# Second channel product of six of eight batches by Strassen's block method, with the later part of the kernel's order made anew

## The chip, the cores and the metric

The kernel runs on one core of one Trainium2 chip. The core has a matrix engine (TensorE, PE in the profile; its weight loads are the row PEld), a vector engine (VectorE, DVE), a scalar engine (ScalarE, ACT), a general engine (GpSimd, POOL) and a queue engine that issues transfers (SyncE, SP). They run side by side and wait for one another by semaphores; each works through its own instructions in the order written. Matmuls read SBUF and write PSUM, which has 8 banks of 128 x 512 f32. The metric is the device time of one execution in microseconds; the median of several runs is compared.

## The reference, cut to what matters

```
kv  = einsum('bhsd,bhse->bhde', k, v)       # q, k, v are (8, 8, 576, 64)
out = einsum('bhsd,bhde->bhse', q, kv)
x   = out / sqrt(mean(out*out, -1) + 1e-6) * g_norm     # then heads side by side: (8, 576, 512)

a1  = alpha1 * x + beta1
tok = einsum('ts,bsd->btd', w_tok, a1)      # 576 x 576 over the tokens
u   = x + lam * tok
a2  = alpha2 * u + beta2
ch  = maximum(a2 @ w_ch1, 0) @ w_ch2        # 512 -> 2048 -> 512
out = u + lam * ch                          # f32, (8, 576, 512)
```

The change is in the second factor of `ch`: per batch a product of 576 x 2048 (after the maximum) by 2048 x 512.

## The kernel before, in words

A batch b (0 to 7) has 576 tokens: four full chunks of 128 tokens (c = 0 to 3, the main rows) and 64 left over. The left-over rows of an even batch and of the odd one after it are put together into one chunk of 128 (c = 4, the tail), which is worked with the odd batch.

The stages of a batch, with the lines that the profile names:

- kv (lines 611, 617): per pair of heads, matmuls of k with v in a slow fp32 form; ACT and DVE put the result into `kvc` (628, 630). The q rows are transposed by DVE in `qs` to `qp` (1093) and copied by ACT into `qt` (1096).
- norm (701, five chunks): q times kv, four slow fp32 matmuls each, then ACT squares (669), DVE sums (672), ACT root, DVE reciprocal, and three DVE products of 512 columns (680, 685, 687), the last two into `rm` (bf16, for the token mix) and `xm` (f32, kept).
- tok (784; tail 829): the token mix, five bf16 matmuls of 512 columns per chunk; DVE adds the result to `xm` (794).
- a2: two POOL operations per chunk (874 by alpha2, 881 plus beta2, to bf16 in `a2b`), then a transposing DMA on SP into `a2m` (three buffers).
- ch1 (894): for each of 16 blocks fj of the 2048 features, four matmuls of 512 columns; ACT takes the maximum with 0 into `ht[:, fj, :]` (889). The tail has 64 matmuls of 128 columns (906).
- ch2 (923): for each chunk c, 16 matmuls of 512 columns, with a 128 x 128 block of `ht` as weights and `w2[:, fj, :]` streamed. Then `finish`: DVE multiplies the bank by lam into `tmp` (951), POOL adds it to `xm` (956; on DVE in the last batch), SP stores the rows (960; tail 964). In the last batch, chunk 3 comes last and in three parts of 256, 128 and 128 columns (934), so that little follows the last matmul.

Every operation is made by a call of `P.op`, `P.mm` or `P.dma` and gets a number in the order of the calls. `ORDER` is a written list of these numbers, made by a planner: `replay` puts the operations in this order, and each engine's and each queue's instructions follow it. "722:1" gives the operation's PSUM bank; numbers joined by "+" have their matmuls interleaved one by one (`woven`), which is how the slow fp32 matmuls of attention are set between bf16 ones. `GATES` are extra dependences, mostly for loads. `synchronize` works out the waits. The costs that the planner used are lines of the kernel: VectorE 0.155 us + n/960, ACT 0.175 + n/1200, POOL 0.08 + 2.42 n/1000 for two operands.

POOL also issues the loads of k and v of the next batch (1083, 1087), SP those of q (1075).

Of the kernel before, what the change touches and what calls it, by code (L numbers as in the profile page):

```python
# [6 lines left out]
F32 = mybir.dt.float32  # L7
F32R = mybir.dt.float32r
# [16 lines left out]
13 0 3 6 30 4 31 ~32 14 7 1 32 12 9 28 5 8 208 10 36 11 27 21 37 35 20 34 29 19 49 43:1 48 ~5 18  # L25
26 16 50:2 25 15 17 2 52:4 56:5:6 51 ~3 57 53 44 23 54:3 45:7 58 62 59 22 63 60 64 55 61 65
127:1 46 73:4:5 38 128 66:2:3 74 42 129 80:6 75 67 190 137:1:7 24 189 81 68 76 191 77 138 82 69
192 130 70 78 40 83 39 ~2 71 135:5 79 143 131:4 139 136 144 140 133:2 145 84 141 85 132 87:5 88
~3 146 99:6 86 142 111:3 112 134 33 113 100 101 114 105:7 106 89 207 102 196 93:4 94 116 107 90
# [1175 lines left out]
```

## Time and profile before

| | us |
|---|---|
| runs | 343.48, 345.99, 346.15 |
| median | 345.99 |
| span of the profiled execution, first to last instruction | 341.3 |
| TensorE busy in it | 332.7 |

For the profiled execution the span is what is given; the times of runs hold what lies around the span, too. In the rows of groups, a line reads: line of the kernel, engine, operation, output <- inputs, shapes, count; then busy time in us and the mean ns of one; then the idle time of the engine before them, and what ended it. A mean of matmuls includes the run through the array, which overlaps the next matmul's, so the pitch from start to start is shorter than the mean. In a timeline or a chain, a line begins with its start and its length in us. In a table by stretch, a line reads: stretch, length, busy time (and count) of PE, PEld, DVE, ACT and POOL, the granted clock of TensorE, the DMA share and GB/s.

### The profile page before, as it was taken

The page shows a single profiled execution, that of the slowest core. Times are in us where ns is not written, and L with a number is a line of the kernel's source. Part 1 is how long each engine was busy: PE and PEld are TensorE (multiplying, and loading weights), DVE is VectorE, ACT ScalarE, POOL GpSimd, SP SyncE. Part 2 cuts the span into 40 slices and gives each one's busy share as a digit, 9 for nine tenths or more (in the row PEclk, how much of TensorE's full clock was granted, in tenths as well). Part 3 has the DMA queues.
Part 4 walks back from the last instruction along what each step waited for, and adds up shares of the span by engine and source line. Part 5 has one row for each costly group of instructions (what it writes and reads, how often), then busy time and mean ns, then how long its engine had stood idle before and what let it go on. Part 6 is the DMA issues. An engine that isn't in the chain of part 4 may idle for free.

```text
span 341.3 us, 5403 instructions
## 1 busy us (share of the span) xinstructions
PE 332.7 (97%) x2141; PEld 191.0 (56%) x2177; DVE 185.9 (54%) x346; ACT 148.8 (44%) x302; POOL 162.3 (48%) x154
## 2 busy tenths in 40 slices
PE   7999999999999999999999999999999999999996
PEld 7776653556555544555655555554576444444644
DVE  3694098424985796365744794458624963210044
ACT  5763663148603680336503572336325472026400
POOL 3699057572039608761087706932292607930000
PEclk9999999999999999999999999999999999999999
DMA  7999999999913991379723995399407530330013
GB/s 261 304 271 230 211 197 298 121 139 276 119 35 62 243 215 23 93 168 236 136 33 76 257 197 72 95 138 246 79 0 125 187 105 17 77 129 12 0 63 92
DMA packets 108496, 48.10 MB, mean 141 GB/s; under 512 B 82029, under 2 KB 101557, under 8 KB 108472
## 3 DMA queue, kind: packets, MB, share of 16 engines
q1 hardware_dynamic: 81648, 26.38, 40.6%
q0 software_dynamic: 26800, 21.38, 39.5%
q8 instruction: 17, 0.28, 0.4%
q14 instruction: 7, 0.06, 0.1%
q10 hardware_dynamic: 24, 0.01, 0.0%
HBM read 38.82 MB, written 9.44 MB: 141 GB/s over the span
## 4 chain that ended last, share of the span: by engine, by line
PE 79%; DVE 8%; DMA 4%; ACT 3%; SPq 2%; POOL 2%; issue 1%
PE ps L923 32%; PE ps L894 26%; PE ps L784 8%; PE ps L906 3%; DMA qs<-in_q_dram 3%; PE ps L701 2%; PE ps L611 2%; POOL a2b L881 2%; DMA w<-in_k_dram 1%; DVE ps L680 1%; DVE small L672 1%; PE ps L829 1%; SPq L1075 1%; PE ps L934 1%; PE ps L567 1%
## 5 line engine op out<-in xcount | busy, mean ns | idle before, releaser
L923 PE MATMUL ps<-w,hh 128*128 128x512 bf16 x543 | 134.1, 382 | 0.8 <-issue 0.2
L894 PE MATMUL ps<-a2m,w 128*128 128x512 bf16 x498 | 120.4, 381 | 0.6
L889 ACT ACTIVATE hh<-ps 128x512 bf16<-128x512 f32 x144 | 80.9, 598 | 71.0 <-PE ps L894 58.3
L923 PEld LDWEIGHTS ps<-w,hh 128*128 128x128 bf16 x560 | 48.2, 98 | 50.1 <-issue 0.8
L894 PEld LDWEIGHTS ps<-a2m,w 128*128 128x128 bf16 x512 | 46.5, 98 | 51.3 <-ACT hh L889 1.3
L874 POOL TENSOR_TENSOR a1f<-xm,a_bc 128x512 f32<-128x512 f32 x24 | 30.3, 1270 | 81.4 <-DVE xm L794 81.1
L951 DVE TENSOR_TENSOR tmp<-ps,lam_bc 128x512 f32<-128x512 f32 (+2 forms) x38 | 24.6, 658 | 52.6 <-PE ps L923 46.4
L956 POOL TENSOR_TENSOR xm<-xm,tmp 128x512 f32<-128x512 f32 x28 | 35.3, 1270 | 28.0 <-DVE tmp L951 28.0
L701 PE MATMUL ps<-kvc,qt 128*128 128x128 f32 x140 | 47.7, 406 | 0.7 <-ACT qt L1096 0.7
L881 POOL TENSOR_TENSOR a2b<-a1f,b_bc 128x512 bf16<-128x512 f32 x32 | 40.2, 1270 | 2.7 <-DVE a1f L878 1.8
L611 PE MATMUL ps<-vr,kr 128*128 128x128 f32 x112 | 38.2, 408 | 0.0
L672 DVE TENSOR_REDUCE small<-sq 128x8 f32<-128x512 f32 (+1 forms) x35 | 23.5, 677 | 24.5 <-ACT sq L669 24.0
L701 PEld LDWEIGHTS ps<-kvc,qt 128*128 128x128 f32 x140 | 27.4, 196 | 8.8 <-ACT qt L1096 0.9
L1096 ACT ACTIVATE qt<-qp 128x576 fp32r<-128x576 f32 x24 | 15.9, 679 | 36.9 <-DVE qp L1093 36.9
L669 ACT ACTIVATE sq<-ps 128x512 f32<-128x512 f32 (+1 forms) x35 | 20.5, 594 | 22.7 <-PE ps L701 22.6
L784 PE MATMUL ps<-rm,wt 128*128 128x512 bf16 x109 | 29.3, 381 | 0.9 <-DVE rtl L685 0.7
L794 DVE TENSOR_TENSOR xm<-ps,xm 128x512 f32<-128x512 f32 x24 | 16.3, 688 | 24.4 <-PE ps L784 23.4
L1093 DVE STREAM_TRANSPOSE qp<-qs 128x576 f32<-128x576 f32 x24 | 18.1, 765 | 13.2 <-ACT qt L1096 8.5
L611 PEld LDWEIGHTS ps<-vr,kr 128*128 128x128 f32 x112 | 22.0, 196 | 5.5
L680 DVE TENSOR_TENSOR ps<-ps,small 128x512 f32<-128x512 f32 (+1 forms) x35 | 23.8, 692 | 0.5
L687 DVE TENSOR_TENSOR xm<-ps,g_bc 128x512 f32<-128x512 f32 x28 | 18.6, 677 | 0.2
L906 PEld LDWEIGHTS ps<-a2l,w 128*128 128x128 bf16 x256 | 15.9, 98 | 3.8 <-ACT hh L889 0.2
(125 smaller groups left out, 295.7 us busy)
## 6 DMA issues: line engine op xcount, KB each, us to landing
out_dram<-xm SPq DMA_DIRECT2D x31, 256.0 KB, 2.7
kr<-in_k_dram POOLq DMA_DIRECT2D x7, 1024.0 KB, 8.2
vr<-in_v_dram POOLq DMA_DIRECT2D x7, 1024.0 KB, 10.0
qs<-in_q_dram SPq DMA_DIRECT2D x24, 288.0 KB, 7.2
w<-in_moe_w_ch_dram POOLq DMA_DIRECT2D x8, 512.0 KB, 9.4
xm<-in_q_dram SPq DMA_DIRECT2D x8, 288.0 KB, 5.2
qs<-in_v_dram SPq DMA_DIRECT2D x4, 288.0 KB, 5.5
w<-in_k_dram SPq DMA_DIRECT2D x4, 288.0 KB, 5.6
```

Source lines behind the costliest of these rows:

```text
L611: P.mm("fill", 128, [lambda e, t=t, c=c, h=h, o=128 * (h % 4): e.matmul(t.ap()[:, o:o + 128], kr4[:, h, c:c + 2, :].rearrange("p c d -> p ...
L672: P.op("DVE", dve(n), lambda e: e.tensor_reduce(out=st, in_=sq[rs, s3, 0:nst, :], axis=AX.X, op=ALU.add), r=[("sq", s3)], w=[("sm", s4)])
L680: P.op("DVE", dve(n), lambda e: e.tensor_tensor(out=grp(ps()), in0=grp(ps()), in1=st[..., None].to_broadcast([rs.stop - rs.start, nst, DH] ...
L701: P.mm("fill", 128, [lambda e, p=p: e.matmul(dst(p), qt[:, p, cs], kvc[:, i, p, :], start=(p == 0), stop=(p == 3)) for p in range(4)], r=[ ...
L784: P.mm("fill", 512, [lambda e, sc=sc: e.matmul(t.ap(), wt[:, sc if sc < 4 else tw(b), 128 * c:128 * c + 128], rsrc(b, sc, al), start=(sc = ...
L874: P.op("POOL", pool(512), lambda e: e.tensor_tensor(out=a1f[:, s], in0=x, in1=a2_bc[:], op=ALU.mult), r=ks + ["a2"], w=[("a1f", s)])
L881: P.op("POOL", pool(512), lambda e: e.tensor_tensor(out=a2b[:, c], in0=a1f[:, s], in1=b2_bc[:], op=ALU.add), r=[("a1f", s), "b2"], w=[("a2 ...
L889: P.op("ACT", act(512), lambda e: e.activation(dst, t.ap(), ACT.Relu), r=[t], w=keys, pri=-1000)
L894: P.mm("main", 512, [lambda e, dj=dj: e.matmul(t.ap(), w1[:, dj, 128 * fj:128 * fj + 128], a2m[:, b % 3, dj, :], start=(dj == 0), stop=(dj ...
L906: P.mm("main", 128, [lambda e, dj=dj, fj=fj: e.matmul(t.ap()[:, 128 * fj:128 * fj + 128], w1[:, dj, 128 * (f4 + fj):128 * (f4 + fj) + 128] ...
L923: P.mm("main", 512, [lambda e, fj=fj, t=t, c=c: e.matmul(t.ap(), (ht[:, fj, 128 * c:128 * c + 128] if c < 4 else hl[:, fj, :]), w2[:, fj, ...
L956: lambda e: e.tensor_tensor(out=x, in0=x, in1=tmp[:, s, a:z], op=ALU.add),
```

## The change

For b = 2 to 7 the main rows of `ch2` are made by Strassen's method in the form with seven products. `ht` (features x tokens) is cut into A11, A21, A12, A22: features 0 to 1023 or 1024 to 2047, tokens 0 to 255 or 256 to 511. `w2` is cut into B11, B21, B12, B22: features by output columns 0 to 255 or 256 to 511. Each product is 16 matmuls of 256 columns (two token chunks by eight feature blocks), in two halves g = 0, 1 of eight matmuls. In the texts they are P1 to P7, in the order of the program:

| | weights x streamed | bank | what follows |
|---|---|---|---|
| P1 | A11 x B11 | ta | ACT copies it to `tmp` |
| P2 | A12 x B21 | tb | DVE adds the copy: rows 0 to 255, columns 0 to 255 |
| P3 | hs x ws2 | ta, on top of P1 | ACT copies it |
| P4 | A11' x t1 | tc | ACT copies it |
| P5 | A21' x B12' | ta, on top | DVE adds the copy of P4: rows 256 to 511, columns 256 to 511 |
| P6 | A12' x B22 | tc, on top of P4 | DVE adds the copy of P3: rows 0 to 255, columns 256 to 511 |
| P7 | A22 x ws1 | ta, on top | DVE multiplies by lam: rows 256 to 511, columns 0 to 255 |

The sums are DVE operations, two halves each, in place but for `hs`: A21(g) = A21 - A11, hs(g) = A22 + A21, and after P1 and P2 have read the old values ("late" sums) A11(g) = hs + A11 and A12(g) = A12 - hs. The sums of weights (t1, ws2, ws1, and B12 - B22 in place of B12) are made once, at b = 2 (`weight_sums`, eight operations); the order puts most of them earlier, in the time of batches 0 and 1. Each operand is 128 x 1024 bf16.

POOL does two operations (times lam, plus `xm`) for three of the four blocks and one for the fourth. Since B12 is changed, the tail of b = 3, 5, 7 is made as 16 matmuls by columns 0 to 255 and 16 by the rest, with one DVE sum of the two halves of `hl` between; in b = 7 the tail comes last of all and takes over the split into 256, 128 and 128 columns. For b from 2 on, ch1 runs its blocks in the order 0, 8, 1, 9, ....

To make room, `a2m` has two buffers for three, `a1f` one for two (after the first mixes), `hs` lies over small tables used at the start, `qt` loses 64 columns of zeros, and t1 lies half in `la_bc`, which is free by then.

Operation numbers after, for reading the order: weight sums 642 to 649; ch1 of b = 2 650 to 681, its Strassen part 682 to 721; for b = 3 Strassen 859 to 898 and the tail 899 to 911; for b = 4 ch1 1002 to 1033, Strassen 1034 to 1073; token mix and a2 of batch 5 977 to 1001; b = 5 Strassen 1211 to 1250; b = 6 1378 to 1417; b = 7 1470 to 1509 and the tail 1510 to 1534. Within a Strassen part the numbers run: A21(0), hs(0), A21(1), hs(1), P1 (two), copy, P2 (two), A11(0), A12(0), A11(1), A12(1), add, POOL (two), P3 (two), copy, P4 (two), copy, P5 (two), add, POOL (two), P6 (two), add, POOL (two), stores, P7 (two), product with lam, POOL, stores.

The core of the diff; of the order, the part around batch 4's Strassen products:

```diff
...
+1078+1028:2 1027 967 975 1030:1 1079 1029 976 977:0 1081 1080 1031 1082 1034 982:7 978 987:3 1085
+979 983 1086 992:2 988 980 1089 997:6 993 984 1090 981 1083 1032:5 998 985 1084 1038:1 1035 1033
+1087 989 1039 986 1036 1088 1041:4 1043 990 1040 1037 1042 1044 994 991 1050 1046 1051 1047 995
+1045 1053:0 1052 999 996 1054 1048 1056 1055 1057 1000 1061 1058 1049 1001 1062 1068 1059 1063
+1069 1064 1099:7+1159:3 1070 1091 1107:2+1161:6 1100 1092 1160 1101 1115:5+1163:4 1108 1093 1102
...
+        def both(op, out, in0, in1, r, w):
+            P.op("DVE", dve(in0.shape[1] * in0.shape[2], 2), lambda e: e.tensor_tensor(
+                out=out, in0=in0, in1=in1, op=op), r=r, w=w)
...
+                t1g = ws4[:] if g else la4
+                both(ALU.subtract, t1g, B12[:, j], B11[:, j], [lo4], [("t1", g)])
+                both(ALU.subtract, ws2[:, j], B22[:, j], t1g, [hi4, ("t1", g)], [("t2", g)])
+                both(ALU.subtract, ws1[:, j], B21[:, j], ws2[:, j], [hi4, ("t2", g)], [("t4", g)])
+                both(ALU.subtract, B12[:, j], B12[:, j], B22[:, j], [lo4, hi4], [lo4])
+
+        def sums(g):
+
+            j = slice(4 * g, 4 * g + 4)
+            both(ALU.subtract, A21[:, j], A21[:, j], A11[:, j], four(g, 0, 0), four(g, 0, 1))
+            both(ALU.add, hs[:, j], A22[:, j], A21[:, j], four(g, 1, 1) + four(g, 0, 1),
+                 [("hs", g)])
+
+        def sums_late(g):
+
+            j = slice(4 * g, 4 * g + 4)
+            both(ALU.add, A11[:, j], hs[:, j], A11[:, j], [("hs", g)], four(g, 0, 0))
+            both(ALU.subtract, A12[:, j], A12[:, j], hs[:, j], [("hs", g)], four(g, 1, 0))
+
+        def product(t, first, at, rhs, keys, stop):
+
+            for g in range(2):
+                P.mm("main", 256, [lambda e, c=c, fj=fj: e.matmul(
+                    t.ap()[:, 256 * c:256 * c + 256], at[:, fj, 128 * c:128 * c + 128], rhs(fj),
+                    start=(first and fj == 0 and c == 0), stop=(stop and fj == 7),
+                    skip_group_check=True)
+                    for c in range(2) for fj in range(4 * g, 4 * g + 4)],
+                    r=keys(g), w=[t])
...
+            js = [8 * m + i for i in range(8) for m in range(2)]
+            for fj in range(4, 16) if b == 0 else range(16) if b == 1 else js:
                 ch1(b, fj)
...
+            else:
+                strassen(b)
+                if b % 2:
+                    ch2_tail(b)
```

More of the change, by code (lines that the diff above doesn't have):

```diff
@@ L527, in e1_rows @@
             P.mm("fill", 4 * DH, [lambda e: e.matmul(
-                tg.ap()[:, 0:DH], one[:], row(4, DH), start=True, stop=True)],
+                tg.ap()[:, 0:DH], one[:], grow, start=True, stop=True)],
                 r=["one", ("row", 4)], w=[tg], tile=4)
@@ L915, in ch2 @@
             tiles = {}
-            if b == NB - 1:
-                order, late = order[:-4], order[-1][0]
             for c, n in order:
@@ L926, in ch2 @@
                     for fj in range(4 * n, 4 * n + 4)],
-                    r=[("w2", n)] + [(hk, fj) for fj in range(4 * n, 4 * n + 4)], w=[t])
+                    r=[("w2", n)] + [("h", fj, c // 2) if c < 4 else ("hl", fj)
+                                     for fj in range(4 * n, 4 * n + 4)], w=[t])
                 if n == 3:
                     finish(b, c, t)
-            if b == NB - 1:
-                for a, z in ((0, 256), (256, 384), (384, 512)):
-                    t = P.bank("main")
-                    for n in range(4):
-                        P.mm("main", z - a, [lambda e, fj=fj, t=t, a=a, z=z: e.matmul(
-                            t.ap()[:, 0:z - a], ht[:, fj, 128 * late:128 * late + 128],
-                            w2[:, fj, a:z], start=(fj == 0), stop=(fj == 15))
-                            for fj in range(4 * n, 4 * n + 4)],
-                            r=[("w2", n)] + [("h", fj) for fj in range(4 * n, 4 * n + 4)],
-                            w=[t])
-                    finish(b, late, t, a, z)
+        A11, A21, A12, A22 = ht[:, 0:8, 0:256], ht[:, 0:8, 256:512], ht[:, 8:16, 0:256], ht[:, 8:16, 256:512]
@@ new lines, in ch2_tail @@
+        def ch2_tail(b):
+            hk = [("hl", fj) for fj in range(16)]
+            t = P.bank("main")
+            for n in range(4):
+                P.mm("main", 256, [lambda e, fj=fj, t=t: e.matmul(
+                    t.ap()[:, 0:256], hl[:, fj, :], w2[:, fj, 0:256], start=(fj == 0),
+                    stop=(b == NB - 1 and fj == 15)) for fj in range(4 * n, 4 * n + 4)],
+                    r=[("w2", n)] + hk[4 * n:4 * n + 4], w=[t])
+            both(ALU.add, hl[:, 8:16], hl[:, 8:16], hl[:, 0:8], hk[0:8], hk[8:16])
+            last = b == NB - 1
+            if last:
+                finish(b, 4, t, 0, 256)
+            for a, z in ((256, 384), (384, 512)) if last else ((256, 512),):
+                o = a
+                if last:
+                    t, o = P.bank("main"), 0
+                for n in range(4):
+                    P.mm("main", z - a, [lambda e, fj=fj, t=t, a=a, z=z, o=o: e.matmul(
+                        t.ap()[:, o:o + z - a], hl[:, fj, :],
+                        w2[:, fj, a:z], start=(last and fj == 0),
+                        stop=(fj == 15)) for fj in range(4 * n, 4 * n + 4)],
+                        r=[("w2", n)] + hk[4 * n:4 * n + 4], w=[t])
+                if last:
+                    finish(b, 4, t, a, z)
+            if not last:
+                finish(b, 4, t)
@@ L1052, in bass_transnormer_attn__then__resmlp_affine_kernel @@
         rws = [("row", i) for i in range(6)]
-        alias([("a2m", i, c) for i in (1, 2) for c in range(4)], rws)
+        alias([("a2m", 1, c) for c in range(4)], rws)
         P.readers.setdefault(("a2m", 0, 0), [])
@@ L1161, in bass_transnormer_attn__then__resmlp_affine_kernel @@
                     ch1(b, fj, ts[fj], [3])
-            for fj in range(0 if b else 4, 16):
+            if b == 2:
+                alias([("t1", 0)], ["la"])
+                alias([("hs", i) for i in range(2)],
+                      rws + [("row", 4), ("cst", 0), ("cst", 1), ("a1f", 1)])
+                weight_sums()
+            js = [8 * m + i for i in range(8) for m in range(2)]
+            for fj in range(4, 16) if b == 0 else range(16) if b == 1 else js:
                 ch1(b, fj)
```

153 lines of the change are left out of this document (118 added, 35 removed), and 140 rows, old and new, of tables (GATES, ORDER).

## The prediction

> **What bounds the kernel now.** The page of the profile comes first, for the busy time of each engine and the chain that ended last; then busy time by stretch, each about one batch long.
>
> ```profile
> span 341.3 us, 5403 instructions
> PE 332.7 (97%) x2141; PEld 191.0 (56%) x2177; DVE 185.9 (54%) x346; ACT 148.8 (44%) x302; POOL 162.3 (48%) x154
> PE 79%; DVE 8%; DMA 4%; ACT 3%; SPq 2%; POOL 2%; issue 1%
> ```
> ```profile
> 74.00:112.00 38.00, 37.08 (x246) 22.21 (x249) 24.17 (x44) 18.34 (x38) 17.48 (x16) 1.00 0.99 125
> ...
> 150.00:188.00 38.00, 37.75 (x247) 22.27 (x251) 21.44 (x38) 17.51 (x36) 18.62 (x17) 1.00 0.81 124
> 188.00:226.00 38.00, 37.90 (x209) 20.51 (x212) 23.58 (x41) 17.22 (x34) 21.48 (x19) 1.00 0.93 152
> ```
>
> TensorE is busy 97% of the span and 99% of the middle stretches (37.75 of 38), at full clock (the 1.00). So columns that TensorE need not stream come off the time one for one, as long as it isn't made to wait. In the same stretches VectorE works 21 to 24 us of 38 and GpSimd 18 to 21: they have room on average, and the question is what they do to the order's tight places. The sum starts from this execution; its 341.3 us lie 4.7 below the median of the runs (345.99), and I carry those 4.7 along as what lies around the span.
>
> **TensorE's work.** The pitch of each shape is read in the chain of waits, where nothing but TensorE stands for long pieces.
>
> ```profile
> 303.76 8.63 PE ps L894 x40
> ...
> 317.58 3.57 PE ps L906 x64
> ...
> 334.96 3.55 PE ps L934 x48
> ```
> ```profile
> L934 PEld LDWEIGHTS ps<-w,hh 128*128 128x128 bf16 x48 | 3.4, 98 | 0.4
> ...
> L934 PE MATMUL ps<-w,hh 128*128 128x128 bf16 x32 | 1.9, 219 | 0.0
> L934 PE MATMUL ps<-w,hh 128*128 128x256 bf16 x16 | 1.9, 272 | 0.0
> ```
>
> 512 columns: 8.63/40 = 0.2158 us. 128 columns: 3.57/64 = 0.0558. Line 934 mixes 32 matmuls of 128 columns with 16 of 256: 3.55 - 32 x 0.0558 = 1.765, so 0.1103 each. Two of 256 cost 0.2206 against 0.2158 for one of 512; the 98 ns weight load fits under one of 256, and no row gives a reason for more.
>
> For a batch b = 2 to 7 the main rows take 64 x 0.2158 = 13.81 us now and 7 x 16 x 0.1103 = 12.35 after: 1.46 less, six times 8.76. The tails of b = 3 and 5 become 32 x 0.1103 = 3.53 for 16 x 0.2158 = 3.45: 0.16 back in all. In b = 7 the split last tile moves from rows to the tail: 48 x 0.2158 + 3.45 + 3.55 = 17.36 before, 12.35 + 3.55 = 15.90 after, the same 1.46. Sum: -8.6 us. The fp32 matmuls of attention were woven one to one or one to two with 512-column matmuls; after, always one to one, with the first product or the token mix, never with a block product:
>
> ```profile
> 177.28 0.39 PE L923 MATMUL ps<-w,hh 128*128 128x512 bf16 x1
> ...
> 177.57 0.39 PE L923 MATMUL ps<-w,hh 128*128 128x512 bf16 x1
> ```
>
> One to one, a pair takes 0.29, so the fp32 matmul costs 0.29 - 0.216 = 0.07 and one partner covers it: nothing changes.
>
> **The new sums on VectorE.** Eight more operations per batch (two operands of 128 x 1024 bf16, both in SBUF), three for the odd tails, eight once for the weights.
>
> ```profile
> L956 POOL TENSOR_TENSOR xm<-xm,tmp 128x512 f32<-128x512 f32 x28 | 35.3, 1270 | 28.0 <-DVE tmp L951 28.0
> L951 DVE TENSOR_TENSOR tmp<-ps,lam_bc 128x512 f32<-128x512 f32 x35 | 23.6, 685 | 51.9 <-PE ps L923 46.4 <-remote 2.9 <-POOL xm L956 2.6
> L1093 DVE STREAM_TRANSPOSE qp<-qs 128x576 f32<-128x576 f32 x24 | 18.1, 765 | 13.2 <-ACT qt L1096 8.5 <-DMA qs<-in_q_dram 4.6
> L794 DVE TENSOR_TENSOR xm<-ps,xm 128x512 f32<-128x512 f32 x24 | 16.3, 688 | 24.4 <-PE ps L784 23.4 <-remote 1.0
> ...
> L956 DVE TENSOR_TENSOR xm<-xm,tmp 128x512 f32<-128x512 f32 x3 | 2.1, 692 | 0.1
> ```
> ```profile
> 336.75 0.43 DVE L951 TENSOR_TENSOR tmp<-ps,lam_bc 128x256 f32<-128x256 f32 x1 [0.33 <-PE ps L934]
> ```
>
> No bf16 pair is in the trace. If a 16-bit element costs what a 32-bit one does, 256 to 512 elements adding 0.26 (0.43 to 0.69), 1024 take 0.69 + 0.52 = 1.2 us; if bytes count, they take as long as 512 of f32, 0.69. I take 0.69: the last group above is the only one with both operands in SBUF, and its bytes are the same. The Trainium skill, VectorE: DVE Perf Modes, § The perf-mode tier table, also has 16-bit pairs in SBUF at two elements a cycle; no run here shows it yet. So VectorE gets 8 x 0.69 = 5.5 us more a batch: some 29 of now 36.5.
>
> Does TensorE wait for them? I walked the order by hand through the places where it is tight. Further rows:
>
> ```profile
> 289.85 0.86 PE ps L829 x8
> ```
> ```profile
> 97.08 2.16 PE ps L784 x10
> ```
>
> Batch b = 4, from the start of tok(5, 0): four token tiles of five matmuls at 0.216 (1.08 each) to 4.32; their tail, ten at 0.86/8, to 5.40; the last ch1 group to 6.26; P1 8.02, P2 9.79, P3 11.55, first half of P4 12.43. An operation that reads a bank starts some 0.16 behind the matmuls' slots (272 ns less the 110 of the pitch). VectorE, in the order's sequence: from 1.28 on without a pause the adds of the four token tiles and three transposes (4 x 0.69 + 3 x 0.77) to 6.35, tail add 7.04, hs(0) 7.73, transpose 8.50, A21(1) 9.19, A11(0) 9.88, hs(1) 10.57, A12(0), A12(1) 11.95, the add after P2 12.6, A11(1) 13.3. P3's second half wants hs(1) at 10.67: there. P4's second half wants A11(1) at 12.43: 0.9 late. The same walk gives 0.7 in b = 3 (hs(1)), 0.8 in b = 5 (A11(1)), about nothing in b = 2 (0.1 to spare) and none in 6 and 7, where A11(1) has microseconds in hand. Sum: +2.5 us, with a lower end of nothing, since tenths in my walk decide.
>
> **Other additions.**
>
> ```profile
> L889 ACT ACTIVATE hh<-ps 128x512 bf16<-128x512 f32 x144 | 80.9, 598 | 71.0 <-PE ps L894 58.3 <-PE ps L906 12.2
> ```
> ```profile
> qs<-in_q_dram SPq DMA_DIRECT2D x24, 288.0 KB, 7.2
> ```
>
> Three ACT copies a batch (0.6 each): a product that writes over the copied bank comes one product later, and 1.77 us of matmuls cover the copy; without that cover each would cost some 0.8. GpSimd runs 7 elementwise operations a batch for 4, +3 x 1.27 = 3.8 us, 23 of 36.5. Behind them on GpSimd are the a2 operations of the next mix and the loads of k and v; behind the stores on SP's queue stand the q loads for the next batch, which the order needs some 15 us later and which take 7.2: nothing. Two a2m buffers for three: their former readers, ch1 of two batches before, ended earlier: nothing. Weight sums:
>
> ```profile
> 55.61 0.70 DVE L797 TENSOR_TENSOR ps<-ps,xm 128x512 f32<-128x512 f32 x1 [0.74 <-PE ps L784]
> ...
> 65.64 0.69 DVE L951 TENSOR_TENSOR tmp<-ps,lam_bc 128x512 f32<-128x512 f32 x1 [2.90 <-remote]
> ```
>
> One stands in the hole of 0.74, four (2.8) in the hole of 2.9, the others later: nothing, and up to 1.4 if they hold up GpSimd's chain there.
>
> **The end.**
>
> ```profile
> 337.61 2.08 SPq L960 DMA_DIRECT2D out_dram<-xm  x4
> ...
> 338.86 0.29 DVE L956 TENSOR_TENSOR xm<-xm,tmp 128x128 f32<-128x128 f32 x1
> ```
>
> SP takes 2.08/4 = 0.52 to issue a store. Now one store follows the last add; after, three (both halves of the last slice and one left over): +1.0.
>
> Total: 341.3 - 8.6 + 2.5 + 1.0 = 336.2, and 4.7 around it: **341 us**.
>
> **Rivals.** First, and on the other side: a VectorE operation with both operands in SBUF and a GpSimd operation cannot read SBUF together, and each waits for the other to end. Before, VectorE's operations beside GpSimd have one operand in SBUF:
>
> ```profile
> 214.93 0.65 DVE L794 TENSOR_TENSOR xm<-ps,xm 128x512 f32<-128x512 f32 x1
> ...
> 214.96 1.27 POOL L881 TENSOR_TENSOR a2b<-a1f,b_bc 128x512 bf16<-128x512 f32 x1
> ```
>
> Neither is longer than its group's mean (0.69, 1.27). The only operations with two are line 956's on VectorE, at the end, when GpSimd has no work left: the trace says nothing against this rival. Where the walk above is tight, GpSimd has 10 to 17 operations of 1.27 in a row (a2 of the next mix, then the adds). There a sum would first wait 0.6 on average, and a whole 1.27 when it follows another sum. In b = 4 seven sums stand on the path to A11(1): 3 x 0.6 + 4 x 1.27 = 6.9 more; b = 2 has two and two (3.7), b = 5 three and two (4.3), b = 3 three and one (3.1). That is +18 where GpSimd is always busy, +11 at its mean share of 23/36.5: 352 to 359, I take 355. It decides once a sum waits over 0.5 us on average, for then some 19 waits eat the 8.6. The Trainium skill, SBUF — State Buffer, § Who interferes with whom, speaks for it: a VectorE instruction with two SBUF inputs contends with a GpSimd instruction that reads SBUF, and the second to start blocks until the first ends.
>
> Second: bf16 sums take 1.2 us. 0.51 more on each late sum: 1.9 in b = 2, 2.3 in 3, 3.6 in 4, 2.6 in 5, so 341 + 10.4 = 351. Third: the order hides all of the sums and the end: 341 - 3.5 = 337.5.
>
> **How the numbers follow.** The sum as made, with the small waits: 0.38, 338.5 to 344. All hidden (third rival): 0.12, 337 to 338.5. GpSimd and VectorE in each other's way (first): 0.38, 345 to 361, since the one row with two SBUF operands was taken with GpSimd at rest, which leaves it as open as the sum. Slow bf16 (second): 0.12, 347 to 355, since the nearest row prices by bytes. About 1% (3.5 us: 342.5 and 349.5) is what this measurement can tell from no change. Faster: 0.30 of the sum as made, all 0.12 of the third rival and 0.02 of the first, 0.44; within: 0.08 of the sum, 0.06 of the first and 0.02 of the second, 0.16; slower: 0.30 of the first and 0.10 of the second, 0.40. The signs are nearly even; the sum as made and the third rival, which is its lower end, hold half the chance, so 341 stands, with 337 to 344 as its own range. The range over all cases is 337 to 357: it leaves out the upper part of the first rival, some 0.13, and a few in a hundred below.
>
> **What would show it.** Pitch: 16 matmuls of a block product start 0.110 apart. Sums: a mean near 690 ns, and near 690 too for those beside GpSimd; the first rival shows in sums of 1.3 to 2 us there, with gaps of TensorE of 3 to 7 us in b = 2 to 5 whose releaser is a sum; the second in 1.2 us for all of them, also in b = 7 where GpSimd rests. TensorE's idle time in the middle stretches tells the waits: 0.1 to 0.9 us now. Wrong I am above all if one place of the order, which I walked by means, hangs on another step.

## The result, and the profile after

| | median, us | runs | ratio to before, 95% interval |
|---|---|---|---|
| before, measured beside it | 345.47 | | |
| after | 360.56 | 358.59 to 363.0 (4) | 1.0454, 1.0397 to 1.0512 |

The ratio compares means of runs; two of the ten runs of `one_operand` below, 348.52 and 351.82, are left out of its ratio and its median span as slow ones. The change makes the kernel 4.5% slower. 341 was forecast, with 337 to 357 as the range; the first rival had 352 to 359.

The page of the profile after: the span, busy time by engine, and the chain that ended last.

```profile
span 358.5 us, 6172 instructions
...
PE 330.6 (92%) x2469; PEld 223.4 (62%) x2497; DVE 238.5 (67%) x400; ACT 159.6 (45%) x320; POOL 201.3 (56%) x176
...
PE 38%; DVE 17%; DMA 16%; POOL 15%; SPq 7%; issue 3%; ACT 2%; POOLq 0%; DVEq 0%
```

TensorE had 79% of the chain before and has 38% now; VectorE and GpSimd, which had 10% between them, have 32%. TensorE's idle time is 28 us of the span where it was 9. Busy time by stretch, three of the seven from 74 to 340 us:

```profile
112.00:150.00 38.00, 35.52 (x240) 23.37 (x242) 32.11 (x50) 17.14 (x33) 25.81 (x21) 1.00 0.96 167
150.00:188.00 38.00, 33.85 (x262) 23.87 (x264) 30.36 (x47) 19.84 (x40) 24.46 (x20) 1.00 0.84 136
...
226.00:264.00 38.00, 35.81 (x228) 23.91 (x230) 28.68 (x47) 16.25 (x33) 23.07 (x19) 0.91 0.76 133
```

Two things are new here. TensorE stands idle 2 to 4 us in every stretch from 112 us on, and in the last one shown its granted clock, 1.00 throughout before, has a mean of 0.91. VectorE and GpSimd are busier than the added operations account for: over the span VectorE's busy time grew by 52.6 us for 54 more operations, which at 0.69 are 37, and GpSimd's by 39.0 for 22 more, which at 1.27 are 28. The block sums are all on line 945. Minimum, median and maximum of one in ns, by form, for batches 2 to 7 (the first row has the three sums of the tails too); then how long TensorE's matmuls waited for them, us and times:

```profile
L945 DVE TENSOR_TENSOR hh<-hh x15: 642/692/1665, 128.2 to 352.0; 128x1024 bf16<-128x1024 bf16 x15
L945 DVE TENSOR_TENSOR hs<-hh x12: 682/692/1746, 130.2 to 334.8; 128x1024 bf16<-128x1024 bf16 x12
L945 DVE TENSOR_TENSOR hh<-hs,hh x12: 676/1455/1768, 139.0 to 336.0; 128x1024 bf16<-128x1024 bf16 x12
L945 DVE TENSOR_TENSOR hh<-hh,hs x12: 669/1172/1764, 141.4 to 338.2; 128x1024 bf16<-128x1024 bf16 x12
...
  PE ps L978: 9.5, 4
```

One operation on one shape takes anything from 0.64 to 1.77 us. The timeline of batch 3 shows when it is long:

```profile
181.39 1.72 POOL L890 TENSOR_TENSOR a2b<-a1f,b_bc 128x512 bf16<-128x512 f32 x1
...
181.91 1.75 DVE L945 TENSOR_TENSOR hs<-hh 128x1024 bf16<-128x1024 bf16 x1
...
183.18 1.59 POOL L883 TENSOR_TENSOR a1f<-xm,a_bc 128x512 f32<-128x512 f32 x1
183.69 1.64 DVE L945 TENSOR_TENSOR hh<-hs,hh 128x1024 bf16<-128x1024 bf16 x1
...
183.71 1.05 PE L978 MATMUL ps<-ws,hs 128*128 128x256 bf16 x8 [2.01 <-DVE hs L945]
...
184.74 1.71 POOL L1007 TENSOR_TENSOR xm<-xm,tmp 128x512 f32<-128x512 f32 x1
```

VectorE and GpSimd are both busy without a pause, and their operations end by turns: a GpSimd operation at 183.11, the sum beside it at 183.66, the next GpSimd operation at 184.77, the next sum at 185.33. From one end to the next it is 0.55, 1.11 and 0.56 us, less than the 0.68 and 1.27 that a sum and a GpSimd operation take undisturbed, but counted from their own starts the operations last 1.6 to 1.75. TensorE's third product wants hs(1) at 181.7 and gets it at 183.7. The like happens in batch 2 (a wait of 1.99), batch 4 (2.08, and 1.77 for a copy that was held up) and batch 5 (3.38), and not in 6 and 7. Batch 7 has a wait of another kind: its first matmul of ch1 waits 2.05 at 320 us for the transposing transfer of the mix, four of whose GpSimd operations took 1.60 to 1.68. In `one_operand` below that wait is 0.4.

In batch 4 the clock comes on top (stretch, length, busy time of PE and the others; the third number from the end is the granted clock):

```profile
222.50:225.00 2.50, 0.84 (x8) 0.50 (x6) 2.50 (x4) 1.12 (x2) 2.34 (x3) 1.00 0.25 52
225.00:227.50 2.50, 1.05 (x8) 0.70 (x8) 2.50 (x2) 0.05 (x1) 2.42 (x2) 0.97 0.26 52
227.50:230.00 2.50, 1.77 (x9) 1.28 (x10) 2.50 (x3) 0.00 (x0) 1.72 (x2) 0.50 0.27 56
230.00:232.50 2.50, 2.50 (x13) 1.56 (x12) 1.64 (x3) 0.60 (x1) 1.38 (x1) 0.50 0.00 0
```

Five microseconds with TensorE busy for 1.9, and then it gets half its clock for some 6 to 7: 13 matmuls in 2.5 us where full speed gives 22. That costs about another 3. The clock falls a second time behind the wait of 3.38 in batch 5 (a mean of 0.67 from 270 to 275 us), for about 1.6.

Two smaller differences, the end and the loads of k and v for batch 5:

```profile
353.08 3.68 SPq L1115 DMA_DIRECT2D out_dram<-xt  x6
...
354.28 0.29 DVE L1107 TENSOR_TENSOR xt<-xt,tmp 128x128 f32<-128x128 f32 x1
```
```profile
156.20 0.92 POOL L1234 DMA_DIRECT2D vr<-in_v_dram  x1
...
166.00 0.30 PE L618 MATMUL ps<-vr,kr 128*128 128x128 f32 x1 [2.02 <-ACT small L682]
```

From the last add to the end of the span it is 358.5 - 354.57 = 3.9 us; before, 341.3 - 339.15 = 2.2. And the key and value product of batch 5 waits 2.0. The releaser named, a root on ScalarE, had ended at 165.0; the load of v issued at 156.20 takes 9.7 us to land, which is 165.9, and the product begins at 166.0. Before, the loads of that batch were issued from 152.8 on and their product began at 171.9.

### The profile page after: what moved, and what is told of

Same layout as the page of the kernel before. It is cut to its first block, busy times and chain, and to the rows that moved or that the text cites. A ratio compares the mean times of both kernels' runs of the same rounds, so it can differ in the third digit from the quotient of the medians.

```text
span 358.5 us, 6172 instructions
## 1 busy us (share of the span) xinstructions
PE 330.6 (92%) x2469; PEld 223.4 (62%) x2497; DVE 238.5 (67%) x400; ACT 159.6 (45%) x320; POOL 201.3 (56%) x176
## 4 chain that ended last, share of the span: by engine, by line
PE 38%; DVE 17%; DMA 16%; POOL 15%; SPq 7%; issue 3%; ACT 2%; POOLq 0%; DVEq 0%
PE ps L903 15%; PE ps L978 10%; DMA qs<-in_q_dram 7%; POOL a2b L890 6%; DVE hh L945 4%; POOL a1f L883 4%; DMA vr<-in_v_dram 3%; SPq L1111 3%; SPq L1226 3%; DVE qp L1244 3%; PE ps L792 2%; PE ps L929 2%; DMA w<-in_moe_w_ch_dram 2%; PE ps L915 2%; DMA a2m<-a2b 2%
## 5 line engine op out<-in xcount | busy, mean ns | idle before, releaser
L903 PE MATMUL ps<-a2m,w 128*128 128x512 bf16 x495 | 126.3, 384 | 4.0 <-DMA a2m<-a2b 2.0
L978 PE MATMUL ps<-w,hh 128*128 128x256 bf16 x384 | 46.0, 278 | 0.1
L709 PE MATMUL ps<-kvc,qt 128*128 128x128 f32 (+1 forms) x140 | 42.6, 406 | 0.9 <-ACT qt L1247 0.9
L978 PEld LDWEIGHTS ps<-w,hh 128*128 128x128 bf16 x384 | 38.1, 100 | 7.7 <-issue 0.8
L1004 POOL TENSOR_TENSOR tmp<-tmp,lam_bc 128x512 f32<-128x512 f32 x18 | 24.5, 1361 | 21.8 <-DVE tmp L1016 21.8
L929 PE MATMUL ps<-w,hh 128*128 128x512 bf16 x139 | 34.7, 382 | 0.2
L679 DVE TENSOR_REDUCE small<-sq 128x8 f32<-128x512 f32 (+1 forms) x35 | 23.3, 674 | 13.1 <-ACT sq L676 12.8
L709 PEld LDWEIGHTS ps<-kvc,qt 128*128 128x128 f32 (+1 forms) x140 | 27.2, 195 | 3.0 <-ACT qt L1247 1.1
L1012 ACT ACTIVATE tmp<-ps 128x512 f32<-128x512 f32 x18 | 10.7, 595 | 40.2 <-PE ps L978 40.2
L1016 DVE TENSOR_TENSOR tmp<-ps,tmp 128x512 f32<-128x512 f32 x18 | 12.3, 683 | 24.5 <-PE ps L978 24.5
L978 PE MATMUL ps<-ws,hh 128*128 128x256 bf16 x144 | 19.2, 287 | 5.4 <-DVE hh L945 5.4
```

What stands on the lines that cost most here:

```text
L709: P.mm("fill", 128, [lambda e, p=p: e.matmul(dst(p), qt[:, p, cs], kvc[:, i, p, :], start=(p == 0), stop=(p == 3)) for p in range(4)], r=[ ...
L903: P.mm("main", 512, [lambda e, dj=dj: e.matmul(t.ap(), w1[:, dj, 128 * fj:128 * fj + 128], a2m[:, b % 2, dj, :], start=(dj == 0), stop=(dj ...
L929: P.mm("main", 512, [lambda e, fj=fj, t=t, c=c: e.matmul(t.ap(), (ht[:, fj, 128 * c:128 * c + 128] if c < 4 else hl[:, fj, :]), w2[:, fj, ...
L978: P.mm("main", 256, [lambda e, c=c, fj=fj: e.matmul(t.ap()[:, 256 * c:256 * c + 256], at[:, fj, 128 * c:128 * c + 128], rhs(fj), start=(fi ...
L1004: P.op("POOL", pool(512), lambda e: e.tensor_tensor(out=two(tmp[:, s]), in0=two(tmp[:, s]), in1=lam(f), op=ALU.mult), r=[("tmp", s), "lam" ...
```

## The experiments

The theory after this reading: two-operand sums on VectorE and GpSimd's operations exclude each other, and this is nearly all of the loss. Against it: the sums are late by the order itself; GpSimd's three more operations a batch are what hurts; the clock fell for its own reason.

### Is it an exclusion at all

`lock_alone` computes nothing of the reference: phases of twelve operations on VectorE, on GpSimd, or both at once.

```diff
+phase(lambda e, i: e.tensor_tensor(out=dc[:, i], in0=da[:], in1=db[:], op=TT), None)
+phase(None, lambda e, i: e.tensor_tensor(out=pc[:, i], in0=pa[:], in1=pb[:], op=TT))
+phase(lambda e, i: e.tensor_tensor(out=dc[:, i], in0=da[:], in1=db[:], op=TT),
+      lambda e, i: e.tensor_tensor(out=pc[:, i], in0=pa[:], in1=pb[:], op=TT))
...
```

> A kernel of its own that measures the disputed thing by itself and leaves the computation out: eight stretches of 12 operations on VectorE and 12 on GpSimd, which start together. Theory (two SBUF operands of VectorE and the reads of GpSimd exclude each other): a bf16 sum takes 0.69 us alone and 1.4 to 1.8 beside GpSimd's two-operand operations, which go from 1.27 to about 1.7; the same for an f32 sum of 512; a sum with one operand in PSUM and a reduction stay at 0.69 and 0.67 and leave GpSimd at 1.27; beside a fill on GpSimd, which reads nothing, the sum stays at 0.69; beside a copy of one operand it is stretched. Rival (plain shortage of SBUF bandwidth): every VectorE operation beside GpSimd is stretched by some tenth, whatever its operands. Rival (nothing of its own; the stretching comes from semaphores in the kernel): 0.69 and 1.27 everywhere.

By line: the sum alone, a GpSimd operation alone, both at once (two rows), then the sum with one operand in PSUM beside GpSimd, the sum beside a GpSimd fill, and beside a GpSimd copy.

```profile
L311 DVE TENSOR_TENSOR dc<-da,db x12: 680/681/692, 6.2 to 12.8; 128x1024 bf16<-128x1024 bf16 x12
L312 POOL TENSOR_TENSOR gb<-pa,pb x12: 1259/1260/1262, 13.5 to 26.9; 128x512 f32<-128x512 f32 x12
L313 DVE TENSOR_TENSOR dc<-da,db x12: 692/1743/1750, 28.2 to 45.5; 128x1024 bf16<-128x1024 bf16 x12
L314 POOL TENSOR_TENSOR gb<-pa,pb x12: 1706/1706/1766, 28.3 to 46.7; 128x512 f32<-128x512 f32 x12
L315 DVE TENSOR_TENSOR dc<-ps,fb x12: 677/677/691, 48.4 to 55.0; 128x512 f32<-128x512 f32 x12
...
L319 DVE TENSOR_TENSOR dc<-da,db x12: 681/683/692, 83.4 to 90.0; 128x1024 bf16<-128x1024 bf16 x12
...
L321 DVE TENSOR_TENSOR dc<-da,db x12: 691/1519/1522, 94.2 to 109.2; 128x1024 bf16<-128x1024 bf16 x12
```

Side by side both engines go at about 1.7 us an operation: 12 pairs in 20.2 us, hardly better than one after the other (12 x 1.94 = 23.3). With one operand in PSUM, or beside a GpSimd operation that reads nothing, the sum is as fast as alone; beside a copy, which reads one input, it takes 1.52. So it is two SBUF inputs against GpSimd's reads, and each is held up by the other. That two f32 inputs of 512 columns fare the same (1.744) shows that it is not a matter of bf16.

### How much of the loss it is

`one_operand` puts a reduction of the same length and with one SBUF input in the place of each of the 48 sums. The sums are left out by that, so the products take the blocks as they are. `thin_pool` keeps the sums and has GpSimd's elementwise operations from batch 2 on work on 8 of the 512 columns; `thin_pool_before` does the same to the kernel before.

```diff
-            both(ALU.subtract, A21[:, j], A21[:, j], A11[:, j], four(g, 0, 0), four(g, 0, 1))
+            one_in(hw[:, 0:8, 128:256][:, j], four(g, 0, 0), four(g, 0, 1))
...
+            P.op("DVE", dve(512), lambda e: e.tensor_reduce(
+                out=scr[:, i], in_=src, axis=AX.X, op=ALU.max), r=r, w=w)
```
```diff
+            nn = 512 if b < 2 else 8
...
-                out=a2b[:, c], in0=a1, in1=b2_bc[:], op=ALU.add),
+                out=a2b[:, c, 0:nn], in0=a1[:, 0:nn], in1=b2_bc[:, 0:nn], op=ALU.add),
```

> The changed kernel with each of the 48 sums of ht replaced by a reduction over the same block read as 512 f32 (one operand in SBUF, 0.67 us, the length that the sum has alone); P3 takes A22 for hs. The sums are so left out; waits, order and GpSimd's work are as in the changed kernel. Theory (exclusion of two-operand reads): no operation is stretched, 340 to 345 us, as the forecast's own sum had it. Rival (VectorE is simply too full, and the order's places too tight, whatever an operation reads): 355 to 361, as the changed kernel. In between, 346 to 354, both have a part.

> The changed kernel with GpSimd's elementwise operations from batch 2 on cut from 512 columns to 8 (a2, the product with lam, the adds to xm; the other columns are left out). Theory: with next to nothing to collide with, the sums take 0.69, and the time is 337 to 343. Rival (VectorE too full): 354 to 361, since VectorE has as much to do as before.

> The control: the kernel before with the same cut of GpSimd's operations from batch 2 on. Both theories: 343 to 347, since TensorE is busy 99% there and waits for GpSimd nowhere; if it comes out below 342, GpSimd's operations cost time before as well, and the run of the changed kernel with the same cut has to be read against this one.

| | median, us (runs) | ratio to before, 95% interval | span of the profiled execution, us |
|---|---|---|---|
| one_operand | 346.68 (10) | 1.0031, 0.9991 to 1.0071 | 343.0 |
| thin_pool | 340.29 (4) | 0.9856, 0.9794 to 0.9918 | 339.6 |
| thin_pool_before | 344.69 (10) | 0.9992, 0.9958 to 1.0026 | 340.9 |

The reductions of `one_operand`, beside a GpSimd as busy as in the kernel after (group of the line, mean in ns), and what TensorE still waits for:

```profile
L967 DVE TENSOR_REDUCE hs<-hh 128x4 f32<-128x512 f32 x48 | 31.1, 674 | 17.8 <-ACT hh L899 17.3
```
```profile
PE ps L619 <- issue: 2.5, 1, 2.5
PE ps L619 <- DVE small L686: 1.9, 1, 1.9
```

All 48 at 674 ns, and 15.5 of the 17.2 us of span that the change cost are gone; by the medians of the runs it is 13.9 of 15.1. The reductions stand in the sums' places in the order and GpSimd has all its operations, so neither the order nor GpSimd's three more operations a batch made this part. 346.68 is nevertheless above the 340 to 345 expected: two products that need k and v (line 619 here) wait, in batches 5 and 7, and the clock falls behind the second.

In `thin_pool` no sum is stretched:

```profile
L946 DVE TENSOR_TENSOR hh<-hs,hh x12: 650/682/693, 137.5 to 317.1; 128x1024 bf16<-128x1024 bf16 x12
```

With GpSimd thinned, the change is worth 1.4%, and the thinning itself is worth nothing to the kernel before: there GpSimd was nobody's bound. The two kernels with a thin GpSimd also show the saved columns by themselves (the one made from before first):

```profile
PE 334.5 (98%) x2177; PEld 191.0 (56%) x2177; DVE 185.7 (54%) x346; ACT 148.8 (44%) x302; POOL 81.7 (24%) x154
```
```profile
PE 327.5 (96%) x2497; PEld 222.6 (66%) x2497; DVE 219.4 (65%) x400; ACT 159.8 (47%) x320; POOL 91.5 (27%) x176
```

7.0 us less of TensorE's busy time (its half clock after a wait for loads, 1.5, is in the second). The spans of these two executions differ by only 1.3, but the first was the quickest of its ten runs (342.85) and the second the longest of its four (341.92); the medians differ by 4.4.

### The clock by itself

In `thin_pool`, too, the clock falls once, behind a wait of 2.0 for the loads of batch 7. `clock_alone` computes nothing of the reference; it runs blocks of 120 matmuls of 256 columns behind waits of different length.

```diff
+o = stream(120)
+for n in (1, 2, 3, 4, 5, 6, 8, 12):
+    o = stream(120, [gap(o, n)])
+for n, m in ((2, 9), (2, 36), (1, 9)):
+    for _ in range(4):
+        o = stream(m, [gap(o, n)])
+    o = stream(120, [gap(o, n)])
```

> A kernel that computes nothing of the reference: blocks of 120 matmuls of 256 columns (13 us), parted by single waits of growing length for a chain of 1, 2, 3, 4, 5, 6, 8 and 12 VectorE copies (some 0.5 to 9 us); then four waits for two copies with 1 us of matmuls between, four with 4 us between, four waits for one copy with 1 us between, each series ahead of a block of 120. Theory (the clock falls because TensorE waited): short waits leave 1.00; from a wait of 3 to 4 us on the clock falls to 0.5 for 6 to 7 us, so that 60 matmuls after it take 0.22 each in place of 0.11; the close series fall too, those with 4 us between don't. Rival (the fall in the kernel has another cause): 0.11 a matmul and 1.00 in all of it.

The timeline has the length of each block and the wait ahead of it:

```profile
76.74 13.27 PE L288 MATMUL ps<-fil 128*128 128x256 bf16 x120 [2.37 <-DVE dst L296]
...
92.85 14.94 PE L288 MATMUL ps<-fil 128*128 128x256 bf16 x120 [2.83 <-DVE dst L296]
...
111.54 16.08 PE L288 MATMUL ps<-fil 128*128 128x256 bf16 x120 [3.75 <-DVE dst L296]
...
158.25 14.94 PE L288 MATMUL ps<-fil 128*128 128x256 bf16 x120 [0.98 <-DVE dst L296]
...
194.52 13.28 PE L288 MATMUL ps<-fil 128*128 128x256 bf16 x120 [0.98 <-DVE dst L296]
```

Single waits of 0.5 to 2.4 us leave the block at 13.27; waits of 2.8, 3.8 and 5.6 add 1.7, 2.8 and 2.2. The block at 158.25 came behind five waits of 0.98 with 1.2 of work between, and lost 1.7; the one at 194.52, with 4.1 of work between the same waits, lost nothing. Five waits of 0.52, 1.2 of work apart, lost nothing either. So the fall is a consequence of the waits, and here it makes a single wait from 2.83 us on 1.4 to 1.75 times as dear. My expectation had the edge at 3 to 4 and the half clock at 6 to 7 us; the edge is lower, and the half clock lasts 3 to 6 (a loss of 1.7 to 2.8, doubled). Each of these was run once, and in the kernels the length of the wait alone does not decide: the clock fell behind 1.96 (`thin_pool`) and 1.85 (`one_operand`), and stayed at 1.00 behind 1.99, 2.02 and 2.01 (after) and 2.52 (`one_operand`). What else decides is not shown.

### Fewer operations on GpSimd, in the kernel itself

`fold_alpha` computes the reference: alpha2 goes into the rows of the first product's weights, once, on ScalarE, and GpSimd adds beta2/alpha2 in one operation a tile instead of two (alpha2 must not be zero for that). `fold_both` puts lam into the second product's weights as well, so that VectorE adds blocks to `xm` straight from PSUM.

```diff
+    P.op("ACT", act(512, 2), lambda e, wv=wv, dj=dj: e.activation(
+        wv, wv, ACT.Identity, scale=a2c[:, dj:dj + 1]), r=["col"], w=[("w1", i)], tag=...)
...
-                out=a2b[:, c], in0=a1, in1=b2_bc[:], op=ALU.add),
+                out=a2b[:, c], in0=x if t is None else a1, in1=b2_bc[:], op=ALU.add),
```
```diff
+    P.op("DVE" if n == 3 else "POOL", pool(512), lambda e, fj=fj: e.tensor_tensor(
+        out=w2[:, fj, :], in0=w2[:, fj, :], in1=lam_bc[:], op=ALU.mult), ...)
...
+                out=X[:, cs, f], in0=two(t.ap()), in1=X[:, cs, f], op=ALU.add),
```

> Alpha2 is multiplied into the rows of the first product's weights once (sixteen ScalarE operations of 0.6 between the first products of batches 1 and 2) and beta2 divided by alpha2, so that the mixes of batches 2 to 7 need one GpSimd operation a tile in place of two: 27 of GpSimd's operations go, 11.5 a batch are left of 16, and those that go stand in the tight places. Nothing else is changed. Theory (the sums collide with GpSimd, and this is nearly all of the loss): the collisions fall by a third to a half, 351 to 355. Rival (the order itself, the end and the clock make the loss, GpSimd little): 359 to 361.

> As fold_alpha, and lam is multiplied into the second product's weights after batch 1 (twelve operations on GpSimd, four on VectorE, once; the weight sums made after it), so that VectorE adds a block straight from PSUM to the output: GpSimd has no lam operation and three adds a batch in place of four, 7.5 operations a batch in all; VectorE has as many as before, one less for each odd tail. Theory: about half of the collisions of the tight places are left of those that fold_alpha leaves, 343 to 349, with one to three of it lost around the scaling before batch 2. Rival: 356 to 360.

`fold_alpha` came to 354.29 (ratio 1.0284, 1.0236 to 1.0331), as the theory had it: 27 operations of 1.27 less on GpSimd, 6.3 us less. Whether these stood in the way of sums or were late themselves, this run alone does not tell; `one_operand` does. `fold_both` came to 364.68 (1.0591, 1.0531 to 1.065), far from either expectation. Its stretches say where:

```profile
112.00:150.00 38.00, 26.26 (x116) 12.90 (x117) 31.12 (x47) 17.49 (x35) 23.86 (x21) 0.86 0.76 152
150.00:188.00 38.00, 36.52 (x255) 25.35 (x257) 26.29 (x43) 17.52 (x35) 14.11 (x12) 0.96 0.74 131
```

The scaling of w2 and the weight sums behind it take VectorE and GpSimd just ahead of batch 2, the norm of the next batch is late by that, and TensorE stands idle 12 us in one stretch, with a mean clock of 0.86 on top; from there on it waits no more than in `fold_alpha`. As a test of the collisions it is spoilt by its own start, and as a version it is no good.

`end_two_queues` is the kernel after with the first two of the last six stores issued from ScalarE.

```diff
-                    P.dma("SP", "ot%d%d" % ((b // 2) % 2, i), dcost(64, 86), lambda e, i=i:
+                    P.dma("ACT" if (z, a) == (256, 0) else "SP", ...
```

> After, with the first two of the last six stores issued from ScalarE's queue. If the six stores one after another on SP set the end: 1.2 less than after (two issues of 0.6). If the stores' landing or the adds set it: no change.

361.0 (1.0474, 1.0403 to 1.0546), no different from after. The issue queue:

```profile
354.82 1.18 ACTq L1116 DMA_DIRECT2D out_dram<-xt  x2
...
355.81 2.41 SPq L1116 DMA_DIRECT2D out_dram<-xt  x4
```

The four left on SP still go one behind the other, from the second add on, and it was these that set the end: the two that went were out of the way in time anyway. From last add to end it is 3.7 in place of 3.9. With four of the six on ScalarE, in `order_alone` below, it is 3.2.

### The order, and both together

TensorE's waits in `fold_alpha` named further places: a copy of q behind the scalings on ScalarE (1.6), and these two (timeline; a reciprocal on VectorE, which held up the norm by 2.6, and the product for batch 5):

```profile
88.12 3.34 DVE L1327 RECIPROCAL a_bc<-a_bc 128x512 f32<-128x512 f32 x1
...
170.81 0.45 PE L628 MATMUL ps<-vr,kr 128*128 128x128 f32 x1 [4.50 <-issue]
```

The division by alpha2 holds VectorE for 3.3 us, and the wait for k and v, with the sums faster, has grown to 4.5. `fold_alpha_2` moves the division and six of the sixteen scalings, sets that product some 4 us later, and issues four of the last stores from ScalarE:

```diff
-912:0+833:1 ... 913+835:2 ... 914:5+837:4 ... 915+787:1 ... 916+792:2 ... 797:4 ... 802:6 ... 864
+833:1 ... 835:2 ... 837:4 ... 912:0+787:1 ... 913+792:2 ... 914:5+797:4 ... 915+802:6 ... 916+864
```

> As fold_alpha, with three places mended that its waits name: the division by alpha2 stands where VectorE is idle (1.3 to 2.6 us of TensorE's wait), six of the sixteen weight scalings behind the transposes of q of batch 3 (1.6 us), and the key and value product of batch 5 goes beside the token mix of batch 4, some 4 us later, so that its loads have landed (a wait of 4.5 us, and the half clock after it, some 3 us); four of the last six stores are issued from ScalarE's queue (up to 1.2). If the waits are independent of each other: 354.3 less 9 to 12, 342 to 345. If only the exclusion counts and the waits move on to the next place: 350 to 354.

351.35 (1.0194, 1.0157 to 1.0232): not the 342 to 345 of independent waits, but waits that move on. The mended waits were gone or under 1 us, but the division now held up blocks of batch 0 (2.8 us of wait), and those for sums had grown (2.4 in batch 3 where it was 0.8, 2.0 in batch 5 where it was 1.75). So the next step was the order of the sums. `sums_first` is the kernel after with VectorE's queue changed in batches 2 to 5: the transposes of q for the batch after next go behind the sums (for batch 3):

```diff
-868 ... 921 ... 923 ... 872 ... 925 ... 927 ... 869 ... 862 ... 870 ... 871
+862 ... 868 870 ... 872 ... 869 871 921 923 ... 925 927
```

`fold_alpha_3` is `fold_alpha_2` with this order and the division behind those blocks; `order_alone` is `fold_alpha_3` without the folding.

> After, with VectorE's order alone changed in batches 2 to 5: the four transposes of q for the batch after next (and ScalarE's copies of them), which stand between the block sums, come behind them, and the sums that the fourth product needs come ahead of those for the sixth. Same operations. Theory: the sums still take up to 1.75 beside GpSimd, but start 2 to 3 us sooner against the products that need them; most of the 9.5 us that TensorE waits for sums and the half clock of batch 4 go: 349 to 354. Rival (the sums meet GpSimd's operations wherever they stand, and what is saved comes back later in the same batch): 357 to 361.

> As fold_alpha_2, with the division by alpha2 moved again, behind the last block of batch 0 that it held up (2.8 us of wait there), and with the order of sums_first. Its waits for sums were 1.4, 2.4, 0.6, 0.2 and 2.0. If these go: 351.35 less 6 to 9, 342 to 345, level with before. If they move on instead: 347 to 351.

> Fold_alpha_3 without its folding of alpha2: after's operations, all sixteen of GpSimd's a batch among them, with the order of sums_first, the key and value product of batch 5 some 4 us later, and four of the last stores from ScalarE's queue. Sums_first (353.5) left waits of 3.5 for that product's loads, of 3.8 for a copy and of 2.1 for a mix's transfer. Theory (order and collisions each have a share): the wait of 3.5 and a half clock after it go, the others stay, 346 to 350, so that 5 to 9 of fold_alpha_3's gain are GpSimd's fewer operations. Rival (the place of the sums and of the loads is all that matters): 341 to 344.

| | median, us (runs) | ratio to before, 95% interval | span of the profiled execution, us |
|---|---|---|---|
| sums_first | 353.5 (4) | 1.0249, 1.0205 to 1.0294 | 351.4 |
| order_alone | 347.16 (12) | 1.0074, 1.0046 to 1.0102 | 345.4 |
| fold_alpha_3 | 341.35 (6) | 0.9898, 0.9854 to 0.9942 | 341.5 |

In `sums_first` the sums are as slow as they were (same columns as for line 945 above), but no block product waits for one any more; TensorE's longest waits are now:

```profile
L944 DVE TENSOR_TENSOR hh<-hs,hh x12: 683/1468/1758, 136.4 to 328.9; 128x1024 bf16<-128x1024 bf16 x12
```
```profile
PE ps L977 <- ACT tmp L1011: 3.8, 2, 2.8
PE ps L617 <- issue: 3.5, 1, 3.5
PE ps L902 <- DMA a2m<-a2b: 2.1, 1, 2.1
```

`sums_first` lies at the upper end of its 349 to 354. The second of these waits goes in `order_alone`, the first and third stay: a copy and a mix's transfer; its 347.16 is as the theory had it, with a share for each, and 5.8 more come with the folding. In `fold_alpha_3`, where GpSimd has fewer operations to be late with, the wait for the copy is down to 1.0, the one for the transfer is gone, and most sums run free:

```profile
PE 326.0 (95%) x2469; PEld 221.3 (65%) x2497; DVE 231.8 (68%) x402; ACT 169.8 (50%) x336; POOL 163.8 (48%) x149
```
```profile
L953 DVE TENSOR_TENSOR hh<-hs,hh x12: 675/684/1755, 139.5 to 319.8; 128x1024 bf16<-128x1024 bf16 x12
L953 DVE TENSOR_TENSOR hh<-hh,hs x12: 675/682/1762, 142.7 to 322.0; 128x1024 bf16<-128x1024 bf16 x12
```

The medians are 0.68 again where they were 1.2 and 1.5, and this version beats both kernels, before by 1.0% (0.6 to 1.5); 341.35 is below the 342 to 345 expected. That this is the columns and not the edits on their own is argued from `thin_pool_before`, which has a far lighter GpSimd without gain; before with alpha2 folded was not run.

## Why the prediction was wrong

**The step that failed** is the sum's term for VectorE's new operations: "So VectorE gets 8 x 0.69 = 5.5 us more a batch", and the walk built on it, "Sum: +2.5 us". The 0.69 is right for a sum alone (0.681 measured), and wrong beside GpSimd, where the walk used it: there sums took up to 1.77, and TensorE waited 9.5 us for them and 1.8 for a copy behind one, where the sum had 2.5 in all. What took its place is the first rival, as it was put: taking the second operand out of SBUF gave back 15.5 us of span (13.9 by the medians of the runs), between the rival's bounds of 11 and 18. The batches it named are those that waited for sums, 6 and 7 did not, and its price for batch 4 (6.9) compares with 3.85 of waiting and about 3 of half clock. For batches 2, 3 and 5 its 3.7, 3.1 and 4.3 compare with 2.0, 2.0 and 3.4: the order had a little more room than the walk gave it. Even without collisions the +2.5 of the walk was too much: in `thin_pool`, where the sums take 0.69, no product waits over 0.2 for one. The Trainium skill, SBUF — State Buffer, § Who interferes with whom, has the rule, and the runs agree with it in each case tried: two SBUF inputs against a GpSimd read block, one input or a GpSimd fill does not.

Why it was chosen wrongly: the sum as made and the rival stood at 0.38 each, and the sum's price came from a row on which the rival's condition (GpSimd at work) did not hold. That row was used as if it spoke for the sum; it could not speak to the question at all, and the only statement that did was against. (The sums that the rival counts on the way are 20, not 19; nothing hangs on it.)

**What the rival lacked** is the clock. Its 355 was made of waits alone, and of these only 11.3 us came, the lower end of its 11 to 18. The half clock after them, about 4.6 in batches 4 and 5, and things that it did not count (loads, the mix's transfer, the end) carry the time past 359. That 355 is so near is in part luck. The Trainium skill, TensorE: Matmul & The Clock Gate, § HAM oscillation — how this bites in real kernels, has gaps of over some 3.4 us as the point where the clock is lost. Here it is lost earlier: after one wait of 2.83 by itself, not after 2.37; in the kernels after 3.85 in two pieces and after 3.38, and behind waits of about 2 sometimes.

**Point by point, the rest.** The pitch held: 32 matmuls of two products in 3.66 us, 32 x 0.1103 and the last one's run through the array. Nothing speaks against the -8.6; the thin pair shows 7.0, with 1.5 of half clock against it. The second rival (1.2 us for a bf16 sum) fell with 0.681. The third (all hidden, 337.5) was where `thin_pool` ought to have come, and didn't: its profiled execution missed 341.3 - 8.6 = 332.7 by 6.9. The end is 1.7 of that where +1.0 was forecast (3.9 from last add to end, `end_two_queues` shows why). The loads of k and v, "nothing" in the prediction, are 2.0 and 1.5 of half clock: in the new order they stand further back on GpSimd's queue. Their tile was free 19 us before the loads of batch 5 were issued in the kernel after, and 22 before those of batch 7 in `thin_pool`, where before it was 12 and 14. And 1.5 is a wait for the first product's weights at 35 us. Of the ten kernels of this form seven have it (0.4 to 1.7) and three have not (`one_operand`, `fold_both`, `fold_alpha_2`), and before has not; its cause was not looked into.

So the account of the profiled executions is: 341.3, less 8.6 of columns, plus 6.9 of start, loads and end, plus 3.4 (343.0 less 339.6) between `thin_pool` and `one_operand`, plus 15.5 of collisions with the clock that fell after them: 358.5. It takes one execution of each kernel, and these do not lie equally near their medians. By the median spans of all runs (before 343.0, `thin_pool` 338.5, `one_operand` 344.7, after 358.8) it is 343.0 - 8.6 + 4.1 + 6.2 + 14.1 = 358.8. The collisions stay by far the largest term; the 4.1 and the 6.2 are differences that no run takes apart. For the second, the trace of `one_operand` has two waits for k and v (2.5 and 1.9) where that of `thin_pool` has one (2.0). The 4.7 around the span was off the other way: the profiled execution of after took 360.25 for a span of 358.5, so what lies around the span is under 2, and most of the 4.7 was the distance of one quick execution of before from the median.

"1.77 us of matmuls cover the copy" failed in one place. In batch 4 the copy of P1 stands on ScalarE's queue behind a copy of q, whose transpose stands on VectorE's behind a sum; TensorE waited 1.77 for an operation of 0.6 that needed nothing but P1.

## What to carry to other kernels

Before work is moved to an engine with room, ask what it shares while it runs: two engines that are busy 67% and 56% of the time, as here, can still be one bound if their operations exclude each other. A row taken while the other engine rested prices nothing beside a busy one; a test with the two of them alone is cheap. And when TensorE starts to wait, count half as much again or more for a wait of about 3 us, for the clock, and expect the gain to come back in pieces, as here: 13.4 us by setting the operations and loads that something waits for ahead of those that nothing does (`order_alone`, with four stores on ScalarE's queue), and 5.8 more by less to collide with (`fold_alpha_3`).

## What had not been expected of the hardware

The stretching is nearly symmetric, 1.74 and 1.71 for operations of 0.68 and 1.26, and 12 pairs take 20.2 us of the 23.3 that strict turns would: some of each operation still overlaps. TensorE's clock was lost after 2.8 us of idle time and after five waits of 1 us with 1.2 us of work between, at a cost of 1.7 to 2.8 us each time; 4.1 us of work between such waits kept it. A reciprocal of 128 x 512 f32 took 3.34 us on VectorE where a product takes 0.69.
